# Softmax attention and a soft mixture of experts on one core: x turned in a slot's first half, denominators and product of x amid the second half's scores, maxima turned ahead of q and k

## The chip, the core and the metric

The kernel runs on one core of a Trainium2 chip. The time is the device time of one execution in microseconds (us). The core has five engines that run their own instructions in order and wait for each other by semaphores: PE (TensorE, matrix products into PSUM), ACT (ScalarE), DVE (VectorE), POOL (GpSimd, which here also issues most DMAs) and SP.

## The reference

```python
scores = scale * q @ k.T                     # 8 batches, 12 heads, 448 tokens, 64 wide
m = max(scores, -1)
e = exp(scores - m)
attn = e / (sum(e, -1) + exp(-m) + 1e-9)     # a softmax with one more term in the denominator
x = (attn @ v), heads side by side           # 3584 tokens x 768
logits = x @ phi                             # 32 slots
d = softmax(logits, 0); c = softmax(logits, 1)
out = c @ experts(d.T @ x)                   # 8 experts, relu(. @ w1[e]) @ w2[e]
```

## The kernel before

**Pairs and slots.** The 96 heads are worked on as 48 pairs; the two heads of a pair (hl = 0, 1) lie in partitions 0 to 63 and 64 to 127. After a ramp written out by hand, the loop at L751 has one slot for each pair s, with two halves (y = 0, 1). All order on the engines is the order of the program (a manual schedule); nothing is reordered.

**What is done to a pair n.** T(n) (L243, quads L270) turns q and k with 28 64x64 transposes on PE; ACT copies q out of PSUM, DVE copies k. A(n, i) makes the scores of 128 queries, and DVE takes the maximum over keys (L303, L313, L321) into wm. When the maxima of a group of three pairs are there, W2 turns them on PE (three products 128 wide and two into 64 partitions, L328 and L330), and W3 copies them (mT, L336) and makes exp(-m) in two instructions (ec, L340 and L343). Bk(n, i) makes the transposed scores of key block i, adds minus the maximum with a second product (sel times mT, L365, L394), and ACT takes exp (L367, L397). Inside Bk, in the steps form at L370, the products of A for a pair some slots ahead stand between those of Bk. AV (L431) multiplies with v, whose extra column of ones gives the sums: 64 queries of each head, the tail, go into separate halves of the partitions (shape 128x64), the rest in 128x128. N1 (L444) copies the result into ubuf on ACT. N2 adds exp(-m) to the sums on DVE (L459), takes the reciprocal (L460), and POOL multiplies (L464, L474, L475) into x. PX (L496) turns x on PE with four 128x128 products, and ACT copies it (L502).

**A slot before.** First half: Bk(s, 0), Bk(s, 1), AV of pair s-1 for key blocks 2 and 3, the work of the expert routing listed in post, the tail of AV(s-1), N1(s-1). Second half: Bk(s, 2), Bk(s, 3), T(s+6), in every third slot W2 and W3, AV(s) for key blocks 0 and 1, post, PX(s-2), and N2(s-1). So the product of a pair is started at the end of one slot, and x is turned at the end of the next.

**What else is in the queues.** POOL also does V (copies of v into its layout, L403 to L406), issues the loads of q, k, v and the weights (L176, L179, L183, L184, L113), and does parts of the routing (c_sub L572, d_sub L586, the scaling of acc L602). V and the loads of v come at the end of slots with s % 3 = 0, those of q and k with s % 3 = 2. The routing of a batch element repeats every six slots: l_mm (L530) in the first half of slots with s % 6 = 2, its maxima in slots 2 and 3, exps and corr in slot 4, s_mm (L618) in the second half of slots with s % 6 = 0. W2 falls in the second half of slots 2 and 5.

**Buffers.** PSUM has three banks for psA (scores for the maxima, turned k, routing), four for psB (scores, turned q, turned maxima, turned x), and one for psV (AV).

Of the kernel before, what the change touches and what calls it, by code (L numbers as in the profile page):

```python
# [31 lines left out]
def kernel(  # L32
# [123 lines left out]
    with ExitStack() as at:  # L156
# [86 lines left out]
        def T(n):  # L243
            g, pl = divmod(n, NP)
            if n >= NP * NP:
                quads(n, g, pl)
                return
            ps = psB.tile([128, 2, S], BF16, tag="b", name="ps_t")

            k0 = [psB.tile([128, 2, S], BF16, tag="b", name="ps_k") for _ in range(2)] if n == 0 else None  # L250
            for a in range(2):
                src = nat["qk"[a], g]
                order = [(tok, hl) for tok in range(7) for hl in range(2)]
                if a and n == 0:
                    order.sort(key=lambda z: kcol(z[1], z[0]))
                for tok, hl in order:
                    c = kcol(hl, tok) if a else (2 * tok if tok < 4 else 2 * tok - 7) * 64
                    r = slice(64 * hl, 64 * hl + 64)
                    o = k0[c // 256][r, 0, c:c + 64] if a and n == 0 else ps[r, a, c:c + 64]
                    nc.tensor.transpose(o, src[r, pl, tok * D:(tok + 1) * D], ident[r, r])  # L260
            t = qk_t[n % NQK]
            if n == 0:
                nc.scalar.copy(t[:, 0, :], ps[:, 0, :])
                nc.vector.tensor_copy(t[:, 1, 0:256], k0[0][:, 0, 0:256])
                nc.vector.tensor_copy(t[:, 1, 256:S], k0[1][:, 0, 256:S])
            else:
                nc.scalar.copy(t, ps)
            qkT[n] = t

        def quads(n, g, pl):  # L270

            pss = [p.tile([128, S], BF16, tag=tag, name="ps_t") for p, tag in ((psB, "b"), (psA, "a"))]
            for tok in range(7):
                for z in range(2):
                    for a in range(2):
                        hl = (z + a) % 2
                        r, o = slice(64 * z, 64 * z + 64), slice(64 * hl, 64 * hl + 64)
                        c = kcol(hl, tok) if a else (2 * tok if tok < 4 else 2 * tok - 7) * 64
# [3 lines left out]
            nc.vector.tensor_copy(t[:, 1, :], pss[1])  # L282
            qkT[n] = t
# [11 lines left out]
        def A(n, i, steps=False):  # L295
            t = qkT[n]
            if steps:

                def run(hl):
                    r = slice(64 * hl, 64 * hl + 64)  # L300
                    ps = psA.tile([128, 512], F32, tag="a", name="ps_a")
                    nc.tensor.matmul(ps[:, 0:S], t[r, 0, i * 128:(i + 1) * 128], t[r, 1, :], start=True, stop=True)  # L302
                    nc.vector.reduce_max(mcol(n, i, hl), ps[:, 0:S], axis=AX.X)  # L303

                return [lambda: run(0), lambda: run(1)]
            if i < 3:
                pss = [psA.tile([128, 512], F32, tag="a", name="ps_a") for _ in range(2)]
                for hl in range(2):
                    r = slice(64 * hl, 64 * hl + 64)
                    nc.tensor.matmul(pss[hl][:, 0:S], t[r, 0, i * 128:(i + 1) * 128], t[r, 1, :],  # L310
                                     start=True, stop=True)
                for hl in range(2):
                    nc.vector.reduce_max(mcol(n, i, hl), pss[hl][:, 0:S], axis=AX.X)  # L313
            else:
                ps = psA.tile([128, 512], F32, tag="a", name="ps_a")

                for hl in range(2):
                    r = slice(64 * hl, 64 * hl + 64)
                    nc.tensor.matmul(ps[64 - 64 * hl:128 - 64 * hl, 0:S], t[r, 0, 384:448], t[r, 1, :],  # L319
                                     start=True, stop=True)  # L320
                nc.vector.reduce_max(mcol(n, 3), ps[:, 0:S], axis=AX.X)  # L321

# [1 line left out]
        def W2(g):  # L324
            w = wm[g % 2]
            ps = pb_("ps_m")
            for i in range(3):
                nc.tensor.matmul(ps[:, i * 128:(i + 1) * 128], w[:, i, :], ident, start=True, stop=True)  # L328
            for z in range(2):
                nc.tensor.matmul(ps[64 * z:64 * z + 64, 384:448], w[:, 3, 0:64], ident[:, 64 - 64 * z:128 - 64 * z],  # L330
                                 start=True, stop=True)
            st["ps_m"] = ps

        def W3(g):
            t = psm.tile([128, S], BF16, tag="mT", name="mT")
            nc.scalar.copy(t, st["ps_m"][:, 0:S])  # L336
            mT[g] = t
            e = psm.tile([128, NP, 7], F32, tag="ec", name="ec", bufs=3)
            w = wm[g % 2]
            nc.scalar.activation(e[:, :, 0:6].rearrange("p l (i h) -> p l i h", i=3),  # L340
                                 w[:, 0:3, :].rearrange("p i (h c) -> p c i h", h=2)[:, 0:NP],
                                 AF.Exp, scale=-scale)
            nc.scalar.activation(e[:, :, 6], w[:, 3, 0:NP], AF.Exp, scale=-scale)  # L343
            ec[g] = e


        def Bk(n, i, c=0, mix=False):
# [4 lines left out]
            if i < 3 and mix and runs and runs[0][1] < 3:  # L352
# [10 lines left out]

                def bias(hl):
                    nc.tensor.matmul(pss[hl][:, 0:S], sel[rs[hl], pl:pl + 1].to_broadcast([64, 128]),  # L365
                                     mT[mg(n)][rs[hl], :], start=False, stop=True)
# [24 lines left out]
                nc.tensor.matmul(outs[hl], t[rs[hl], 1, cols], t[rs[hl], 0, :], start=True, stop=False)  # L391
            As(c)
            for hl in range(2):
                nc.tensor.matmul(outs[hl], sel[rs[hl], pl:pl + 1].to_broadcast([64, m]), mT[mg(n)][rs[hl], :],  # L394
                                 start=False, stop=True)
            for p, e in zip(pss, es):
                nc.scalar.activation(e, p[:, 0:S], AF.Exp, scale=scale)  # L397
# [18 lines left out]
        def AV(n, i, qs):  # L416
# [6 lines left out]
            for u in qs:  # L423
                for hl in range(2):
                    if u < 3:
                        c0 = (2 * u + hl) * W65
                        o, qc = a[:, c0:c0 + W65], slice(u * 128, (u + 1) * 128)
                    else:
                        t, z = (av_half["ps"], 0) if n == NPAIR - 1 else (a, 6 * W65)
                        o, qc = t[64 - 64 * hl:128 - 64 * hl, z:z + W65], slice(384, 448)  # L430
                    nc.tensor.matmul(o, eT[n, i, hl][:, qc], vp[g % 2][:, 2 * pl + hl, i, 0:W65],  # L431
                                     start=(i == 0 and u == 0 and hl == 0) or (u == 3 and i == 0 and n == NPAIR - 1),
                                     stop=(i == 3), skip_group_check=True)

# [3 lines left out]
        def N1(n):  # L438
# [5 lines left out]
            (nc.scalar.copy if on_pool(n) else nc.vector.tensor_copy)(u, src)  # L444
            us[n] = u

        def N2(n):
            g, pl = divmod(n, NP)
            b, pb = divmod(n, PB)
            u = us[n]  # L450
            eng = nc.gpsimd if on_pool(n) else nc.vector
            rec = psm.tile([128, 7], F32, tag="rec", name="rec", bufs=3)
            e = ec[mg(n)][:, group[n][1], :]
            if n == NPAIR - 1:
                nc.vector.scalar_tensor_tensor(rec[:, 6:7], av_half["ps"][:, D:W65], 1e-9, e[:, 6:7],
                                               op0=ALU.add, op1=ALU.add)
                nc.vector.scalar_tensor_tensor(rec[:, 0:6], u[:, 0:6, D], 1e-9, e[:, 0:6], op0=ALU.add, op1=ALU.add)
            else:
                nc.vector.scalar_tensor_tensor(rec, u[:, :, D], 1e-9, e, op0=ALU.add, op1=ALU.add)  # L459
            nc.vector.reciprocal(rec, rec)  # L460
            x = xb[b % 2]
            c = pb * 128
# [251 lines left out]
        for word in ramp.split():  # L714
# [7 lines left out]
            elif op == "X":  # L722
                W2(*arg)
                W3(*arg)
            elif op == "V":
                AV(*arg, range(3))
            elif op == "H":
# [23 lines left out]
        for s in range(3, NPAIR + 1):  # L751
            for y in range(2):
                hs = 2 * s + y
                mix = len(runs) > 1 and runs[0][1] == 1 - y
                if mix:
                    Bk(s, 2 * y, mix=True)
                    Bk(s, 2 * y + 1, y, mix=True)
                else:
                    As(1)
                if mix:  # L760
# [9 lines left out]
                    for i in (2, 3):  # L770
                        AV(s - 1, i, range(3))
                else:
                    if s < NPAIR - 6:
                        T(s + 6)
                    if s and s + 1 in firsts:
                        W2(mg(s + 1))
                        W3(mg(s + 1))
                    if s < NPAIR:
                        for i in (0, 1):
                            AV(s, i, range(3))  # L780
                for f in post.get(hs, ()):
                    f()
                if y and 0 <= s - 2 < NPAIR - 2:
                    PX(s - 2)
                if y == 0:
                    if 0 <= s - 1:
                        for i in range(4):
                            AV(s - 1, i, [3])
                        if s == NPAIR:
                            PX(s - 2)  # L790
                        N1(s - 1)
                        if not on_pool(s - 1):
                            N2(s - 1)
                else:
                    if 0 <= s - 1 and on_pool(s - 1):
# [227 lines left out]
```

## Time and profile before

| what | us |
|---|---|
| median of 3 runs (298.39 to 298.96) | 298.4 |
| the profiled execution | 297.51 |
| its span, first to last instruction | 295.7 |
| PE busy | 270.1 |
| ACT busy | 254.0 |
| DVE busy | 247.7 |
| POOL busy | 190.0 |

A busy time is the union of an engine's instructions, each with its latency: on ACT and DVE the next instruction starts before the one ahead has ended, and a product on PE shows about 0.16 us of pipeline behind the time in which it streams. In this document the distance between the starts of two neighbouring instructions is therefore used as the time that one of them costs. Six slots of the steady part, by their first product (us from the span's start):

| slot | begins | long | what is special |
|---|---|---|---|
| 29 | 157.05 | 4.98 | W2 and W3 |
| 30 | 162.03 | 5.32 | s_mm |
| 31 | 167.35 | 4.35 | |
| 32 | 171.70 | 5.39 | l_mm; W2 and W3 |
| 33 | 177.09 | 4.67 | routing maxima |
| 34 | 181.76 | 4.33 | exps of the routing |

### The profile page before, as it was taken

The page shows a single profiled execution, that of the slowest core. Times are in us where ns is not written, and L with a number is a line of the kernel's source. Part 1 is how long each engine was busy: PE and PEld are TensorE (multiplying, and loading weights), DVE is VectorE, ACT ScalarE, POOL GpSimd, SP SyncE. Part 2 cuts the span into 40 slices and gives each one's busy share as a digit, 9 for nine tenths or more (in the row PEclk, how much of TensorE's full clock was granted, in tenths as well). Part 3 has the DMA queues.
Part 4 walks back from the last instruction along what each step waited for, and adds up shares of the span by engine and source line. Part 5 has one row for each costly group of instructions (what it writes and reads, how often), then busy time and mean ns, then how long its engine had stood idle before and what let it go on. Part 6 is the DMA issues. An engine that isn't in the chain of part 4 may idle for free.

```text
span 295.7 us, 12404 instructions
## 1 busy us (share of the span) xinstructions
PE 270.1 (91%) x5191; PEld 155.6 (53%) x5191; DVE 247.7 (84%) x591; ACT 254.0 (86%) x585; POOL 190.0 (64%) x349
## 2 busy tenths in 40 slices
PE   5999999999999999999999999998999999996820
PEld 4445555555565566555655565556555556662100
DVE  5999899999899989999999999998999665537840
ACT  4569999999999999999999999998999988337730
POOL 8682887978786988887788779876786543000000
PEclk9999999999999999999999999999999999998555
DMA  7999999999999999999999999999699979908997
GB/s 134 147 152 207 150 134 166 198 163 198 176 197 156 191 181 205 168 193 177 200 185 188 186 179 182 186 191 197 105 147 201 219 158 262 352 19 304 410 450 326
DMA packets 47223, 58.67 MB, mean 198 GB/s; under 512 B 3008, under 2 KB 40128, under 8 KB 46912
## 3 DMA queue, kind: packets, MB, share of 16 engines
q0 software_dynamic: 40512, 42.29, 90.4%
q1 hardware_dynamic: 6656, 15.60, 13.6%
q8 instruction: 40, 0.66, 0.8%
q14 instruction: 15, 0.12, 0.1%
HBM read 89.16 MB, written 15.14 MB: 353 GB/s over the span
## 4 chain that ended last, share of the span: by engine, by line
PE 64%; ACT 22%; DVE 5%; issue 3%; DMA 1%; DVEq 0%; ACTq 0%
PE ps_av L431 14%; PE ps_a L302 8%; PE ps_b L362 8%; PE ps_b L365 7%; ACT W L397 6%; ACT W L367 6%; PE ps_b L391 5%; ACT W L502 3%; PE ps_b L394 3%; ACT W L281 3%; PE ps_t L279 3%; PE ps_o L916 2%; DVE W L313 2%; PE ps_x L496 2%; PE ps_s L618 2%
## 5 line engine op out<-in xcount | busy, mean ns | idle before, releaser
L303 DVE TENSOR_REDUCE W<-ps_a 128x1 bf16<-128x448 f32 x250 | 138.4, 614 | 5.0 <-PE ps_a L302 2.2
L367 ACT ACTIVATE W<-ps_b 128x448 bf16<-128x448 f32 x250 | 125.9, 643 | 1.2 <-PE ps_b L365 1.0
L302 PE MATMUL ps_a<-W 64*128 64x448 bf16 x250 | 79.4, 352 | 1.0 <-DVE cm L557 1.0
L362 PE MATMUL ps_b<-W 64*128 64x448 bf16 x250 | 72.3, 352 | 1.4
L431 PE MATMUL ps_av<-W 128*128 128x65 bf16 (+1 forms) x1536 | 65.1, 196 | 0.8 <-ACT ubuf L444 0.6
L365 PE MATMUL ps_b<-mT,sel 64*128 64x448 bf16 x250 | 65.0, 350 | 0.5
L431 PEld LDWEIGHTS <-W 128*128 128x128 bf16 (+1 forms) x1536 | 50.2, 100 | 27.8 <-issue 23.4
L464 POOL TENSOR_TENSOR W<-ubuf,rec 128x384 bf16<-128x384 f32 x44 | 36.3, 824 | 38.6 <-DVE rec L460 20.5
L397 ACT ACTIVATE W<-ps_b 128x448 bf16<-128x448 f32 x86 | 48.7, 607 | 2.5 <-PE ps_b L394 2.5
L502 ACT CAST W<-ps_x 128x512 bf16<-128x512 f32 x47 | 31.4, 667 | 2.3 <-PE ps_x L496 2.0
L365 PEld LDWEIGHTS <-sel 64*128 64x128 bf16 x250 | 19.2, 94 | 21.8 <-issue 14.4
L321 DVE TENSOR_REDUCE W<-ps_a 128x1 bf16<-128x448 f32 x48 | 29.6, 616 | 0.8 <-PE ps_a L319 0.8
L444 ACT COPY ubuf<-ps_av 128x455 f32<-128x455 f32 x44 | 27.7, 630 | 0.2
L113 POOL DMA_DIRECT2D W<-in_moe_w_dram x30 | 22.6, 756 | 8.0 <-PE ps_b L394 7.7
L302 PEld LDWEIGHTS <-W 64*128 64x128 bf16 x250 | 22.8, 94 | 8.8
L391 PE MATMUL ps_b<-W 64*64 64x448 bf16 (+1 forms) x134 | 26.4, 371 | 0.3 <-ACT W L502 0.2
L281 ACT COPY W<-ps_t 128x448 bf16<-128x448 bf16 x39 | 25.7, 658 | 0.0
L394 PE MATMUL ps_b<-mT,sel 64*64 64x448 bf16 (+1 forms) x134 | 24.7, 353 | 0.0
L279 PEld LDWEIGHTS <-W 64*64 64x64 bf16 x1092 | 20.1, 108 | 8.4 <-issue 2.0
L313 DVE TENSOR_REDUCE W<-ps_a 128x1 bf16<-128x448 f32 x38 | 21.1, 615 | 1.6 <-PE ps_a L310 1.4
L475 POOL TENSOR_TENSOR W<-ubuf,rec 128x128 bf16<-128x128 f32 x44 | 17.5, 398 | 3.7
L496 PE MATMUL ps_x<-ident,W 128*128 128x128 bf16 x192 | 18.7, 219 | 0.2 <-ACT W L472 0.2
(154 smaller groups left out, 460.6 us busy)
## 6 DMA issues: line engine op xcount, KB each, us to landing
W<-in_moe_w_dram POOLq DMA_DIRECT2D x24, 768.0 KB, 9.3
W<-in_v_dram POOLq DMA_DIRECT2D x32, 192.0 KB, 5.9
out_dram<-W SPq DMA_DIRECT2D x2, 2688.0 KB, 9.1
W<-in_q_dram POOLq DMA_DIRECT2D x15, 336.0 KB, 6.6
W<-in_k_dram POOLq DMA_DIRECT2D x26, 168.0 KB, 6.7
stage<-in_moe_w_dram POOLq DMA_DIRECT2D x4, 768.0 KB, 9.5
W<-stage SPq DMA_DIRECT2D x4, 576.0 KB, 6.7
out_dram<-W SPq DMA_DIRECT2D x6, 384.0 KB, 2.7
```

Source lines behind the costliest of these rows:

```text
L281: nc.scalar.copy(t[:, 0, :], pss[0])
L302: nc.tensor.matmul(ps[:, 0:S], t[r, 0, i * 128:(i + 1) * 128], t[r, 1, :], start=True, stop=True)
L303: nc.vector.reduce_max(mcol(n, i, hl), ps[:, 0:S], axis=AX.X)
L362: nc.tensor.matmul(pss[hl][:, 0:S], t[rs[hl], 1, cols], t[rs[hl], 0, :], start=True, stop=False)
L365: nc.tensor.matmul(pss[hl][:, 0:S], sel[rs[hl], pl:pl + 1].to_broadcast([64, 128]), mT[mg(n)][rs[hl], :], start=False, stop=True)
L367: nc.scalar.activation(e[:, hl, :], pss[hl][:, 0:S], AF.Exp, scale=scale)
L391: nc.tensor.matmul(outs[hl], t[rs[hl], 1, cols], t[rs[hl], 0, :], start=True, stop=False)
L394: nc.tensor.matmul(outs[hl], sel[rs[hl], pl:pl + 1].to_broadcast([64, m]), mT[mg(n)][rs[hl], :], start=False, stop=True)
L397: nc.scalar.activation(e, p[:, 0:S], AF.Exp, scale=scale)
L431: nc.tensor.matmul(o, eT[n, i, hl][:, qc], vp[g % 2][:, 2 * pl + hl, i, 0:W65], start=(i == 0 and u == 0 and hl == 0) or (u == 3 and i == ...
L464: eng.tensor_mul(x[:, 0:3, c:c + 128].rearrange("p i (h d) -> p i h d", h=2), u[:, 0:6, 0:D].rearrange("p (i h) d -> p i h d", h=2), rec[: ...
L502: nc.scalar.copy(xT(b, pb), pss[0])
```

## The change

1. In a slot's first half PX(s-2) now stands behind the tail of AV(s-1) and N1(s-1); before it was the last product of the second half.
2. N2 is split into den (L459) and mul (reciprocal and the POOL instructions). While there are maxima to be taken, den(s-1) stands between Bk(s, 2) and Bk(s, 3), and mul(s-1) right behind Bk(s, 3), ahead of T, post and PX.
3. W2 and W3 stand ahead of T instead of behind it. The two products of the tail maxima are 128x128 as the other three; for this the second head's q columns begin with the tail, so that the two heads read mT with an offset of 64, and mT is 512 wide instead of 448.
4. exp(-m) is one instruction (W4) instead of two. It is at the end of the next slot's first half, in the ramp and for the last group right behind W3 or T.

```diff
+        qcol = lambda hl, tok: (2 * tok if tok < 4 else 2 * tok - 7) * 64 if hl == 0 else (2 * tok + 1) * 64 if tok < 3 else (2 * tok - 6) * 64
+        def qcs(hl, i):
+            a = 128 * i + 64 * hl if i < 3 else 384 * (1 - hl)
+            return slice(a, a + (128 if i < 3 else 64))
...
         def W2(g):
             for i in range(3):
-                nc.tensor.matmul(ps[:, i * 128:(i + 1) * 128], w[:, i, :], ident, start=True, stop=True)
-            for z in range(2):
-                nc.tensor.matmul(ps[64 * z:64 * z + 64, 384:448], w[:, 3, 0:64], ident[:, 64 - 64 * z:128 - 64 * z],
-                                 start=True, stop=True)
+                nc.tensor.matmul(ps[:, 64 + i * 128:192 + i * 128], w[:, i, :], ident, start=True, stop=True)
+            for hl in range(2):
+                c, h = 448 * (1 - hl), 64 - 64 * hl
+                nc.tensor.matmul(ps[:, c:c + 64], w.rearrange("p i c -> p (i c)")[:, 384 - 64 * hl:512 - 64 * hl],
+                                 ident[:, h:h + 64], start=True, stop=True)
         def W3(g):
-            t = psm.tile([128, S], BF16, tag="mT", name="mT")
-            nc.scalar.copy(t, st["ps_m"][:, 0:S])
+            t = psm.tile([128, 512], BF16, tag="mT", name="mT")
+            nc.scalar.copy(t, st["ps_m"])
...
+        def W4(g):
+            e = psm.tile([128, NP, 8], F32, tag="ec", name="ec", bufs=3)
+            nc.scalar.activation(e.rearrange("p l (i h) -> p i h l", i=4),
+                                 wm[g % 2].rearrange("p i (h c) -> p i h c", h=2)[:, :, :, 0:NP], AF.Exp, scale=-scale)
...
+                early_den = y and on_pool(s - 1)
                 if mix:
                     Bk(s, 2 * y, mix=True)
+                    if early_den:
+                        den(s - 1)
                     Bk(s, 2 * y + 1, y, mix=True)
+                    if early_den:
+                        mul(s - 1)
+                        early_den = False
...
-                    if s < NPAIR - 6:
-                        T(s + 6)
                     if s and s + 1 in firsts:
                         W2(mg(s + 1))
                         W3(mg(s + 1))
+                    if s < NPAIR - 6:
+                        T(s + 6)
+                    if s + 1 == firsts[-1]:
+                        W4(mg(s + 1))
...
-                if y and 0 <= s - 2 < NPAIR - 2:
+                if y == 0:
+                    for i in range(4):
+                        AV(s - 1, i, [3])
+                    if s < NPAIR:
+                        N1(s - 1)
                     PX(s - 2)
...
                     if not on_pool(s - 1):
                         N2(s - 1)
+                    if 3 < s < firsts[-1] and s in firsts:
+                        W4(mg(s))
+                elif early_den:
+                    N2(s - 1)
```

More of the change, by code (lines that the diff above doesn't have):

```diff
@@ L256, in T @@
                 for tok, hl in order:
-                    c = kcol(hl, tok) if a else (2 * tok if tok < 4 else 2 * tok - 7) * 64
+                    c = (kcol if a else qcol)(hl, tok)
                     r = slice(64 * hl, 64 * hl + 64)
@@ L277, in quads @@
                         r, o = slice(64 * z, 64 * z + 64), slice(64 * hl, 64 * hl + 64)
-                        c = kcol(hl, tok) if a else (2 * tok if tok < 4 else 2 * tok - 7) * 64
+                        c = (kcol if a else qcol)(hl, tok)
                         nc.tensor.transpose(pss[a][o, c:c + 64], nat["qk"[a], g][r, pl, tok * D:(tok + 1) * D], ident[r, r])
@@ L301, in run @@
                     ps = psA.tile([128, 512], F32, tag="a", name="ps_a")
-                    nc.tensor.matmul(ps[:, 0:S], t[r, 0, i * 128:(i + 1) * 128], t[r, 1, :], start=True, stop=True)
+                    nc.tensor.matmul(ps[:, 0:S], t[r, 0, qcs(hl, i)], t[r, 1, :], start=True, stop=True)
                     nc.vector.reduce_max(mcol(n, i, hl), ps[:, 0:S], axis=AX.X)
@@ L309, in A @@
                     r = slice(64 * hl, 64 * hl + 64)
-                    nc.tensor.matmul(pss[hl][:, 0:S], t[r, 0, i * 128:(i + 1) * 128], t[r, 1, :],
+                    nc.tensor.matmul(pss[hl][:, 0:S], t[r, 0, qcs(hl, i)], t[r, 1, :],
                                      start=True, stop=True)
@@ L318, in A @@
                     r = slice(64 * hl, 64 * hl + 64)
-                    nc.tensor.matmul(ps[64 - 64 * hl:128 - 64 * hl, 0:S], t[r, 0, 384:448], t[r, 1, :],
+                    nc.tensor.matmul(ps[64 - 64 * hl:128 - 64 * hl, 0:S], t[r, 0, qcs(hl, 3)], t[r, 1, :],
                                      start=True, stop=True)
@@ L327, in W2 @@
             for i in range(3):
-                nc.tensor.matmul(ps[:, i * 128:(i + 1) * 128], w[:, i, :], ident, start=True, stop=True)
-            for z in range(2):
-                nc.tensor.matmul(ps[64 * z:64 * z + 64, 384:448], w[:, 3, 0:64], ident[:, 64 - 64 * z:128 - 64 * z],
-                                 start=True, stop=True)
+                nc.tensor.matmul(ps[:, 64 + i * 128:192 + i * 128], w[:, i, :], ident, start=True, stop=True)
[3 more added lines that the diff above has]
+                                 ident[:, h:h + 64], start=True, stop=True)
             st["ps_m"] = ps
         def W3(g):
-            t = psm.tile([128, S], BF16, tag="mT", name="mT")
-            nc.scalar.copy(t, st["ps_m"][:, 0:S])
+            t = psm.tile([128, 512], BF16, tag="mT", name="mT")
+            nc.scalar.copy(t, st["ps_m"])
             mT[g] = t
[L338 to L343, printed above, removed]
+        def W4(g):
+            e = psm.tile([128, NP, 8], F32, tag="ec", name="ec", bufs=3)
+            nc.scalar.activation(e.rearrange("p l (i h) -> p i h l", i=4),
+                                 wm[g % 2].rearrange("p i (h c) -> p i h c", h=2)[:, :, :, 0:NP], AF.Exp, scale=-scale)
             ec[g] = e
@@ L365, in bias @@
                     nc.tensor.matmul(pss[hl][:, 0:S], sel[rs[hl], pl:pl + 1].to_broadcast([64, 128]),
-                                     mT[mg(n)][rs[hl], :], start=False, stop=True)
+                                     mT[mg(n)][rs[hl], 64 - 64 * hl:64 - 64 * hl + S], start=False, stop=True)
                     nc.scalar.activation(e[:, hl, :], pss[hl][:, 0:S], AF.Exp, scale=scale)
@@ L393, in Bk @@
             for hl in range(2):
-                nc.tensor.matmul(outs[hl], sel[rs[hl], pl:pl + 1].to_broadcast([64, m]), mT[mg(n)][rs[hl], :],
+                nc.tensor.matmul(outs[hl], sel[rs[hl], pl:pl + 1].to_broadcast([64, m]), mT[mg(n)][rs[hl], 64 - 64 * hl:64 - 64 * hl + S],
                                  start=False, stop=True)
@@ L426, in AV @@
                         c0 = (2 * u + hl) * W65
-                        o, qc = a[:, c0:c0 + W65], slice(u * 128, (u + 1) * 128)
+                        o = a[:, c0:c0 + W65]
                     else:
                         t, z = (av_half["ps"], 0) if n == NPAIR - 1 else (a, 6 * W65)
-                        o, qc = t[64 - 64 * hl:128 - 64 * hl, z:z + W65], slice(384, 448)
-                    nc.tensor.matmul(o, eT[n, i, hl][:, qc], vp[g % 2][:, 2 * pl + hl, i, 0:W65],
+                        o = t[64 - 64 * hl:128 - 64 * hl, z:z + W65]
+                    nc.tensor.matmul(o, eT[n, i, hl][:, qcs(hl, u)], vp[g % 2][:, 2 * pl + hl, i, 0:W65],
                                      start=(i == 0 and u == 0 and hl == 0) or (u == 3 and i == 0 and n == NPAIR - 1),
@@ L445, in N1, with den @@
             us[n] = u
+        recs = {}
         def N2(n):
-            g, pl = divmod(n, NP)
-            b, pb = divmod(n, PB)
+            den(n)
+            mul(n)
+        def den(n):
             u = us[n]
-            eng = nc.gpsimd if on_pool(n) else nc.vector
-            rec = psm.tile([128, 7], F32, tag="rec", name="rec", bufs=3)
-            e = ec[mg(n)][:, group[n][1], :]
+            rec = recs[n] = psm.tile([128, 7], F32, tag="rec", name="rec", bufs=3)
+            e = ec[mg(n)][:, group[n][1], 0:7]
             if n == NPAIR - 1:
@@ L459, in N2, with mul @@
                 nc.vector.scalar_tensor_tensor(rec, u[:, :, D], 1e-9, e, op0=ALU.add, op1=ALU.add)
+        def mul(n):
+            b, pb = divmod(n, PB)
+            u, rec = us[n], recs.pop(n)
+            eng = nc.gpsimd if on_pool(n) else nc.vector
             nc.vector.reciprocal(rec, rec)
@@ L724 @@
                 W3(*arg)
+                W4(*arg)
             elif op == "V":
@@ L782 @@
                     f()
-                if y and 0 <= s - 2 < NPAIR - 2:
-                    PX(s - 2)
[L785 to L790, printed above, removed]
+                if y == 0:
[3 more added lines that the diff above has]
+                        N1(s - 1)
+                    PX(s - 2)
+                    if s == NPAIR:
                         N1(s - 1)
[L792 to L795, printed above, removed]
+                    if not on_pool(s - 1):
                         N2(s - 1)
+                    if 3 < s < firsts[-1] and s in firsts:
+                        W4(mg(s))
+                elif early_den:
+                    N2(s - 1)
                 if y == 0 and wait_loads:
```

## The prediction

> **What bounds the kernel now.** I read the page first. Its busy row shows four engines near full at once, so no single one's work gives the time:
>
> ```profile
> PE 270.1 (91%) x5191; PEld 155.6 (53%) x5191; DVE 247.7 (84%) x591; ACT 254.0 (86%) x585; POOL 190.0 (64%) x349
> ```
>
> Next the waits of each engine: PE's are short (1.4 us the longest in all), and POOL's are for `rec` (20.5 us), so POOL looks free. Then the timeline by engine in the steady part, slots 32 to 35. A slot's tail point, below, is where PE has ended the tail of AV and goes on: 174.41, 179.34, 183.88 and 188.53 us. PE in slots 34 and 35:
>
> ```profile
> 182.88 0.35 PE L302 MATMUL ps_a<-W 64*128 64x448 bf16 x1
> 183.16 0.79 PE L431 MATMUL ps_av<-W 128*128 128x65 bf16 x20
> 183.88 0.36 PE L302 MATMUL ps_a<-W 64*128 64x448 bf16 x1
> ...
> 185.34 0.54 PE L431 MATMUL ps_av<-W 128*128 128x65 bf16 x12
> 185.72 0.22 PE L622 MATMUL ps_ct<-ident,cd 128*128 128x128 bf16 x1
> 185.77 0.39 PE L496 MATMUL ps_x<-ident,W 128*128 128x128 bf16 x4
> 186.09 0.36 PE L302 MATMUL ps_a<-W 64*128 64x448 bf16 x1
> ```
>
> and DVE between slots 33 and 34:
>
> ```profile
> 181.11 0.61 DVE L321 TENSOR_REDUCE W<-ps_a 128x1 bf16<-128x448 f32 x1
> 181.64 0.38 DVE L282 COPY W<-ps_t 128x448 bf16<-128x448 bf16 x1
> 181.94 0.15 DVE L459 SCALAR_TENSOR_TENSOR rec<-ubuf,ec 128x7 f32<-128x7 f32 x1
> 182.13 0.20 DVE L460 RECIPROCAL rec<-rec 128x7 f32<-128x7 f32 x1
> 182.25 3.23 DVE L303 TENSOR_REDUCE W<-ps_a 128x1 bf16<-128x448 f32 x6
> ```
>
> The starts close a ring. The fourth scores of a first half (182.88) reuse the psA bank of the first, so they follow its reduce (182.25) by 0.63. From there PE takes 0.28 to AV and 0.72 to the tail point (183.88), where the first scores of the second half stand. Their reduce begins 0.45 later (the fifth of the six: 0.49 and three times 0.53 after 182.25). DVE then needs two reduces (1.06), the third (0.53), the copy of k (0.30), the denominator (0.19) and the reciprocal (0.12), 2.20 in all, until the first reduce of the next slot. 0.63 + 0.28 + 0.72 + 0.45 + 2.20 = 4.28, and slot 34 takes 4.33. ACT's jobs in such a slot, by distance of starts, are seven exps at 0.42, N1 0.42, q 0.41 and x 0.47: 4.26. So ring and ACT are level, and the dearer slots are longer by their own PE work or by what W3 adds to ACT.
>
> POOL is another matter. This is its timeline over slots 32 to 35:
>
> ```profile
> 176.61 0.41 POOL L572 TENSOR_TENSOR z<-lb,cm 128x128 f32<-128x128 f32 x1
> 177.72 0.82 POOL L464 TENSOR_TENSOR W<-ubuf,rec 128x384 bf16<-128x384 f32 x1 [0.70 <-DVE rec L460]
> ...
> 179.37 0.82 POOL L176 DMA_DIRECT2D W<-in_q_dram  x1
> ...
> 181.94 0.79 POOL L113 DMA_DIRECT2D W<-in_moe_w_dram  x1
> ...
> 184.28 0.66 POOL L403 COPY W<-W 128x576 bf16<-128x576 bf16 x1
> ...
> 187.75 0.66 POOL L602 TENSOR_TENSOR acc<-acc,corr 128x224 f32<-128x224 f32 x1
> 188.37 0.82 POOL L464 TENSOR_TENSOR W<-ubuf,rec 128x384 bf16<-128x384 f32 x1
> 189.54 0.40 POOL L475 TENSOR_TENSOR W<-ubuf,rec 128x128 bf16<-128x128 f32 x1
> ```
>
> From the product of pair 31 (177.72) to the end of that of pair 33 (189.94) it has no idle time. PX(33) begins at 190.75, 0.81 later: all the slack there is.
>
> **The change, part by part.**
>
> PX in the first half. Four turns last 0.32 (185.77 to 186.09) and now stand in the ring, behind the tail point: 0.63 + 0.28 + 0.72 + 0.32 + 0.42 + DVE. On DVE the denominator no longer stands just ahead of the reciprocal that waits for it (0.12 for 0.19; the trace has no denominator followed by a reduce, so 0 to 0.19): 2.13. The ring becomes 4.50, 0.22 more than now, in every slot that it bounds. In the second half AV(s) now meets the scores itself. Where AV is followed by another shape its 12 products take 0.466, where by PX 0.375: PE has one more switch of shape in a slot, 0.09 us.
>
> The Trainium skill's page TensorEngine Tiling (Array Packing), section Tiling Modes, says "Changing tiling mode (not just tile) drains the TensorE", which speaks against this part. The trace agrees (0.466 against 0.375); with PE alone setting the end it would be the first rival below.
>
> Maxima ahead of q and k. B3 to W2, W2 to T and T to AV are three switches; T to W2, to its 128x64 products, to AV were three too: nothing on PE. On ACT, W3 goes from 0.42 to that of a copy 512 wide, 0.47, and two exps (0.13 + 0.09) become one, between 0.13 and 0.23, taken as 0.14, in the next first half: less by 0.03, 17 times, 0.5 us at most. What helps is the order: today x's copy waits behind W3 and both exps, and the next first half's scores take 1.73 to 1.80 instead of 1.40 because the fourth psB bank is x's.
>
> Now the six intervals between tail points from slot 29 on, today and then:
> - 29 to 30 (W2): 5.06; then ACT bounds with N1, x, seven exps, W3, q = 4.72, taken as 4.70.
> - 30 to 31 (s_mm): 4.98; PE's 0.32 + 0.65 + 0.40 + 0.35 + 0.38 + 0.70 + 0.09 = 2.89, then 0.42 + 0.63 + 0.28 + 0.72 = 4.94.
> - 31 to 32 (l_mm, 0.59 in the ring): 4.88; 4.50 + 0.59 = 5.08.
> - 32 to 33 (W2): 4.93; PE's 0.32 + 0.65 + 0.50 + 0.31 + 0.35 + 0.38 + 0.23 = 2.74, then 0.42 + 0.63 + 0.28 + 0.78 = 4.85.
> - 33 to 34: 4.54; ring with 0.12 of s_max in DVE's way, 4.62.
> - 34 to 35: 4.65; ring with the copy of L623, 4.63.
>
> 29.04 becomes 28.82: 0.2 less in six slots, if x's products are in time.
>
> The products on POOL. Today mul starts when the reciprocal is out, 3.16 behind slot 32's tail point. Then: PX 0.32, first reduce 0.42, two reduces 1.06, denominator 0.12, third reduce 0.53, reciprocal 0.20 = 2.65, so 0.51 earlier. But c_sub (176.61), which POOL does today while it waits, then stands behind the product: +0.43. Everything from the q load on is unchanged and without a gap, so pair 33's product ends at 189.94 - 0.51 + 0.43 = 189.86. PX(33) moves from 190.75 to slot 35's tail point, 174.41 + 4.85 + 4.62 + 4.63 = 188.51. **PE waits 1.4 us** with the semaphore. Behind PX stand N1's copy of x on ACT, all second-half scores, their reduces and exps: nothing covers it, and the next slots, near their bounds, can't give it back. The same sum for pairs 21 and 27 gives 1.4 each, with their gapless queues. Pair 39 (no loads of q): 0.9. Pair 9 (no L602): 0.7. Pair 3: 0.4. Pair 15, where the q load waits 1.11 for something else: 1.4 to 2.4, taken as 1.9. Pair 43 in the tail: 0.5. Products that aren't behind V's and q's queue: pair 31's has 0.45 to spare and pair 30's 0.5. Sum: 0.4 + 0.7 + 1.9 + 4.2 + 0.9 + 0.5 = 8.6. Against it 0.2 in some six periods: -1.2.
>
> Net +7.4. The profiled execution took 297.5 (1.8 around its span of 295.7), so 304.9; the median of the runs is 0.9 above it: **305.8 us**.
>
> **The rivals.**
> - PE alone (0.10): the ring is loose, because DVE's order changes and reduces catch up, and products come in time as the slots stretch. Then 0.09 of shape switch in some 42 slots is 3.8: 302.2. For it: PE busy 28.73 of 29.04 us in slots 29 to 34. Against it: its waits are hidden as long first stages of scores.
> - ACT's relief wins (0.10): the one way to a faster kernel. x's copy leaves the second half, and the first stages of 1.73 to 1.80 fall to 1.40 twice in six slots: 0.37 x 13 = 4.8, 293.6. It decides only where POOL ends the third pair's product before the tail point; its gapless 10.6 us from 179.37 speak against it.
> - The change doesn't do what it says (0.06): the reciprocal comes no earlier, held by ec or by scores behind PX; then the stall has 0.51 more in six places: 308.8.
> - Gains and stalls cancel (0.04): 298.4.
> - The forecast has 0.70.
>
> **How the numbers follow.** Lower end of the forecast's own bounds: the stalls stay, but the three intervals without them fall to ACT's 4.26 to 4.7, some 14.0 instead of 14.7: 4 us less over the periods, 301.5. Upper end: every stall full and 0.2 of ring in the intervals that I hold at ACT's bound, 311. The range reaches down to the case of no change: 298.2 to 311.0, and leaves out the faster rival and the forecast's ends. Some 0.6 us (0.2%) is what a measurement can tell from no change. Faster 0.10, same 0.04, slower 0.86.
>
> **What would show it.** In the profile after: PE waiting at L496 for POOL's x, about 1.4 us in slots 11, 17, 23, 29, 35 (a wait that today doesn't exist); first-half scores after a W2 slot at about 1.4 instead of 1.8; plain slots near 4.5; AV of the second half at 0.47. If PE has no such wait, the forecast is wrong, most likely because POOL's work between two products is placed otherwise than I read it. If the waits are there and the total is under 301, it is the rows of the ring that are wrong.

## The result, and the profile after

The changed kernel takes 303.6 us (median of 4 runs, 303.19 to 304.43) where the kernel before took 298.7 beside it (median of 4, 298.39 to 300.55): a ratio of 1.0142, 95% interval 1.0099 to 1.0185. Ratios, here and below, are worked out from the fast executions alone, as some others of the same kernels ran in a slower state. The ratio differs from the quotient of the two medians, 1.0165, which lies inside the interval. The kernel is slower, as forecast, and inside the range; the forecast of 305.8 was 2.2 us too high. The profiled execution took 304.4, the longest of the four.

The busy row of the page, and the chain of work that ended last, followed back from the last instruction:

```profile
PE 273.2 (90%) x5191; PEld 160.8 (53%) x5191; DVE 246.8 (82%) x591; ACT 255.6 (84%) x568; POOL 189.6 (63%) x349
...
PE 64%; POOL 14%; ACT 5%; DVE 5%; issue 4%; DMA 3%; DVEq 0%; POOLq 0%; ACTq 0%
```

The chain of the kernel before was:

```profile
PE 64%; ACT 22%; DVE 5%; issue 3%; DMA 1%; DVEq 0%; ACTq 0%
```

POOL does the same work as before, and is now in 14% of the chain where it had no share. In the view of the line that turns x (L510 in the new numbering), products and weight loads together, idle time in us and how often:

```profile
  POOL W L489: 6.9, 15
  POOL W L478: 2.0, 7
```

PE and its weight load show the same wait twice here, so these are not to be added. The starts of the phases on PE give what it costs: PX takes 0.33 where it doesn't wait, and the tail 0.25. Above that are 0.43 for pair 9, 0.77 for pair 14, 1.05 for 15, 0.79 each for 21, 27 and 33, 0.71 for 39, and 0.27 for two others together: 5.6 us. Slot 35 on PE:

```profile
192.73 0.79 PE L437 MATMUL ps_av<-W 128*128 128x65 bf16 x20
193.65 0.34 PE L510 MATMUL ps_x<-ident,W 128*128 128x128 bf16 x3
194.41 0.23 PE L510 MATMUL ps_x<-ident,W 128*128 128x128 bf16 x1 [0.41 <-POOL W L489]
194.57 0.36 PE L308 MATMUL ps_a<-W 64*128 64x448 bf16 x1
```

AV and its tail would end at 193.44. The first three turns wait for the large product of x (L478, out at 193.59), the fourth for the small one (L489, out at 194.35), and only then come the second half's scores. POOL in the same time, from the product of pair 31 to that of pair 33:

```profile
181.81 0.82 POOL L478 TENSOR_TENSOR W<-ubuf,rec 128x384 bf16<-128x384 f32 x1 [1.72 <-DVE rec L474]
...
183.35 0.40 POOL L586 TENSOR_TENSOR z<-lb,cm 128x128 f32<-128x128 f32 x1
183.69 0.82 POOL L176 DMA_DIRECT2D W<-in_q_dram  x1
...
192.77 0.82 POOL L478 TENSOR_TENSOR W<-ubuf,rec 128x384 bf16<-128x384 f32 x1
...
193.96 0.40 POOL L489 TENSOR_TENSOR W<-ubuf,rec 128x128 bf16<-128x128 f32 x1
```

It is the queue of before, with c_sub now behind the product, and pair 33's product ends 0.9 us behind the place in which PE wants it.

### The profile page after: what moved, and what is told of

Same layout as the page of the kernel before. It is cut to its first block, busy times and chain, and to the rows that moved or that the text cites. A ratio compares the mean times of both kernels' runs of the same rounds, so it can differ in the third digit from the quotient of the medians.

```text
span 302.6 us, 12387 instructions
## 1 busy us (share of the span) xinstructions
PE 273.2 (90%) x5191; PEld 160.8 (53%) x5191; DVE 246.8 (82%) x591; ACT 255.6 (84%) x568; POOL 189.6 (63%) x349
## 4 chain that ended last, share of the span: by engine, by line
PE 64%; POOL 14%; ACT 5%; DVE 5%; issue 4%; DMA 3%; DVEq 0%; POOLq 0%; ACTq 0%
PE ps_av L437 13%; PE ps_a L308 9%; PE ps_b L368 6%; PE ps_b L371 6%; PE ps_b L397 4%; PE ps_x L510 4%; DMA W<-in_k_dram 3%; POOL W L478 3%; PE ps_t L285 3%; PE ps_b L400 3%; PE ps_o L939 3%; DVE W L319 2%; PE ps_s L632 2%; PE ps_h L876 2%; PE ps_l L544 2%
## 5 line engine op out<-in xcount | busy, mean ns | idle before, releaser
L309 DVE TENSOR_REDUCE W<-ps_a 128x1 bf16<-128x448 f32 x250 | 140.6, 619 | 14.7 <-PE ps_a L308 13.3
L373 ACT ACTIVATE W<-ps_b 128x448 bf16<-128x448 f32 x250 | 121.6, 587 | 3.4 <-PE ps_b L371 3.3
L308 PE MATMUL ps_a<-W 64*128 64x448 bf16 x250 | 81.6, 351 | 0.8 <-DVE W L327 0.7
L368 PE MATMUL ps_b<-W 64*128 64x448 bf16 x250 | 67.3, 353 | 0.0
L478 POOL TENSOR_TENSOR W<-ubuf,rec 128x384 bf16<-128x384 f32 x44 | 36.1, 821 | 44.0 <-DVE rec L474 32.9
L403 ACT ACTIVATE W<-ps_b 128x448 bf16<-128x448 f32 x86 | 46.9, 586 | 2.0 <-PE ps_b L400 2.0
L516 ACT CAST W<-ps_x 128x512 bf16<-128x512 f32 x47 | 29.5, 628 | 5.1 <-PE ps_x L510 5.0
L327 DVE TENSOR_REDUCE W<-ps_a 128x1 bf16<-128x448 f32 x48 | 29.7, 619 | 0.7 <-PE ps_a L325 0.7
L371 PEld LDWEIGHTS <-sel 64*128 64x128 bf16 x250 | 22.2, 94 | 12.0 <-issue 3.4
L450 ACT COPY ubuf<-ps_av 128x455 f32<-128x455 f32 x44 | 25.6, 582 | 0.2
L510 PE MATMUL ps_x<-ident,W 128*128 128x128 bf16 x192 | 21.0, 226 | 3.7 <-POOL W L489 2.7
L287 ACT COPY W<-ps_t 128x448 bf16<-128x448 bf16 x39 | 23.9, 612 | 0.0
L319 DVE TENSOR_REDUCE W<-ps_a 128x1 bf16<-128x448 f32 x38 | 21.1, 618 | 1.6 <-PE ps_a L316 1.4
L489 POOL TENSOR_TENSOR W<-ubuf,rec 128x128 bf16<-128x128 f32 x44 | 17.5, 398 | 3.7
L285 PEld LDWEIGHTS <-W 64*64 64x64 bf16 x1092 | 15.5, 108 | 6.1 <-DMA W<-in_k_dram 0.9
```

The costliest lines, as they stand in the source:

```text
L308: nc.tensor.matmul(ps[:, 0:S], t[r, 0, qcs(hl, i)], t[r, 1, :], start=True, stop=True)
L368: nc.tensor.matmul(pss[hl][:, 0:S], t[rs[hl], 1, cols], t[rs[hl], 0, :], start=True, stop=False)
L478: eng.tensor_mul(x[:, 0:3, c:c + 128].rearrange("p i (h d) -> p i h d", h=2), u[:, 0:6, 0:D].rearrange("p (i h) d -> p i h d", h=2), rec[: ...
L510: nc.tensor.matmul(pss[i // 2 if two else 0][:, o:o + 128], x[:, i, c], ident if i < 3 else ident2, start=True, stop=True)
```

## The experiments

There are four theories of the loss: POOL (PE waits for x's product, which POOL's queue makes late), SHAPE (PE changes the shape of its products once more in each slot), RING (PX makes the loop of PE and DVE longer) and PARTS (the other two parts of the change cost the time). What each expects stands with each run. All ratios are to the kernel before, run on the same chip, with 95% intervals. "Six slots" is taken from the profiled execution: the intervals between the starts of the second half's first scores in neighbouring slots, the median of slots 10 to 40 for each slot number modulo 6, and the sum of these six. It is 29.05 us before and 29.99 after the change. It comes from one execution of each kernel, so it is a help beside the ratio and has no interval.

| kernel | ratio | interval | six slots |
|---|---|---|---|
| change | 1.0142 | 1.0099 to 1.0185 | 29.99 |
| maxima alone | 0.9961 | 0.9928 to 0.9995 | 28.90 |
| denominators alone | 1.0012 | 0.9977 to 1.0048 | 28.95 |
| both, PX where it was | 0.9935 | 0.9893 to 0.9977 | 28.80 |
| PX alone | 1.0454 | 1.0381 to 1.0528 | 31.40 |
| change, PX one pair earlier | 1.0027 | 0.9982 to 1.0073 | 29.16 |
| change, loads of v later | 1.0059 | 1.0019 to 1.0099 | 29.73 |
| change, PX between blocks 2 and 3 | 1.0039 | 1.0003 to 1.0074 | 29.36 |
| the same, loads of v later | 1.0001 | 0.9965 to 1.0036 | 29.31 |
| PX one pair earlier, ahead of the tail | 0.9995 | 0.9962 to 1.0029 | 29.31 |
| both, PX between block 3 and T | 0.9963 | 0.9933 to 0.9992 | 29.10 |
| PX one pair earlier, one denominator later | 1.0023 | 0.9982 to 1.0065 | 29.26 |

### PX back in its place

```diff
+                if y and 0 <= s - 2 < NPAIR - 2:
+                    PX(s - 2)
...
-                    if s < NPAIR:
-                        N1(s - 1)
-                    PX(s - 2)
...
```

> The changed kernel with PX back where it was, last in the second half; early denominators and products and the turned maxima stay. Theory POOL (PE waits for x's product because PX stands 2 us earlier in the program while POOL's queue is as long as before): no wait at PX, and the extra shape switch and the longer ring go too, so 298.0 us or less, 296 to 298.5. Rival SHAPE (the loss is the shape switch of 0.09 us in each slot, some 3.8 us): also gone here, 299 to 300, since the rest of the loss is then the other two parts'. Rival PARTS (early denominators or the maxima cost the time): stays over 301.

297.1 us, 0.9935. No wait of PX for POOL is left, and the kernel is faster than before. With the other parts in, the loss comes from PX's place; PARTS falls.

### PX for one pair earlier

```diff
+        def turned(s):
+            if s == 3 or s >= NPAIR - 4:
+                return [] if s == 3 else [s - 2]
+            return [s - 3, s - 2] if s % PB == 1 else [] if s % PB == 2 else [s - 3]
...
-                    PX(s - 2)
+                    for z in turned(s):
+                        PX(z)
```

> The changed kernel with PX at its new place, but for the pair before: x of pair s-3 is turned in slot s (in slots with s % 6 = 1 also pair s-2, in slots with s % 6 = 2 none, so that the routing finds its x; from slot 44 on as in the change). Same number of products, same shape switches, same place on PE; only the wait for POOL goes. POOL: the waits at PX seen in the changed kernel's trace sum to 5.6 us, so 298.0 (297 to 299.5). SHAPE: nothing changes, 303 to 304. Rival RING (PX between the tail of AV and the next scores makes the loop of PE and DVE longer): 303.

300.2 us, 1.0027, where the kernel before took 299.4 beside it; POOL's 297 to 299.5 is missed. Place and shapes are the change's, only the product is an old one (in one slot of six two pairs are turned, in another none), and of 1.42% there remain 0.27%: by the ratios the wait for POOL is 3.4 us of the loss, less than the 5.6 that the waits sum to. In six slots 0.83 us go, where one stall took 0.79. PE in the slot that waited before:

```profile
191.24 0.79 PE L437 MATMUL ps_av<-W 128*128 128x65 bf16 x20
191.96 0.40 PE L510 MATMUL ps_x<-ident,W 128*128 128x128 bf16 x4
192.29 0.36 PE L308 MATMUL ps_a<-W 64*128 64x448 bf16 x1
```

0.33 from PX to the next scores, for 0.92 in the change. SHAPE and RING as the main cause fall. But 1.0027 against 0.9935 stays: another 2.7 us, without any late product. In six slots it is 0.36 (29.16 for 28.80). Not all of it need be PX's place: of the 4.3 us between the spans of the two profiled executions 0.9 lie ahead of slot 4, where this kernel waits twice for loads of k, 0.63 us each, and the one with PX in its old place once, 0.52. Whether the other executions have such waits isn't shown.

### PX alone

```diff
-                if y and 0 <= s - 2 < NPAIR - 2:
-                    PX(s - 2)
...
                         N1(s - 1)
+                        if s < NPAIR:
+                            PX(s - 2)
```

> The kernel before with PX alone moved to the first half, behind N1; denominators and product at the end of the second half as before, maxima behind q and k. POOL: products start some 0.4 us later than in the changed kernel, so the waits are longer by that in six or seven places and x's product is late in more slots: 306 to 309, with PE waiting 1.2 us or more at PX in slots 11, 17, 23, 29, 35. SHAPE: as the changed kernel or less, 302.4. ACT relief without stalls: under 298.

313.1 us, 1.0454: more than expected. The place is as expected (PE in slot 29):

```profile
167.85 0.79 PE L431 MATMUL ps_av<-W 128*128 128x65 bf16 x20
168.90 0.34 PE L496 MATMUL ps_x<-ident,W 128*128 128x128 bf16 x3 [0.26 <-POOL W L464]
169.65 0.23 PE L496 MATMUL ps_x<-ident,W 128*128 128x128 bf16 x1 [0.41 <-POOL W L475]
169.81 0.36 PE L302 MATMUL ps_a<-W 64*128 64x448 bf16 x1
```

The tail could end at 168.57 (AV and tail 0.72), so PE loses 0.9 here, not 1.2. But there are more such slots. What the line that turns x waits for in this kernel (us, times; products and weight loads together):

```profile
  POOL W L475: 10.1, 24
  POOL W L464: 4.7, 12
```

By the starts on PE, as above, the waits at PX sum to 9.8 of the 13.7 us lost: 0.9 each for pairs 15, 21, 27, 33 and 39, 1.34 for pair 14, 0.80 for pair 30, 0.3 to 0.5 for pairs 3, 8, 9, 20, 26, 32 and 43, and less for some others. So x's product is late in more slots, as POOL expected. Where the other 3.9 us go isn't worked out. Moving only the consumer costs three times what moving it with its producer does.

### The turned maxima alone

```diff
-                    if s < NPAIR - 6:
-                        T(s + 6)
                     if s and s + 1 in firsts:
                         W2(mg(s + 1))
                         W3(mg(s + 1))
+                    if s < NPAIR - 6:
+                        T(s + 6)
```

(with the new W2, W3, W4 and q's columns of the change)

> The kernel before with the turned maxima alone: W2 and W3 ahead of T, one shape, one exp in the next first half; PX, denominator and product where they were. Forecast by the trace: first scores after a slot with W2 fall from 1.8 us towards 1.4, some 0.2 to 0.3 us in each of 13 such slots, so 295 to 297.5. If the maxima ahead of T make DVE's or ACT's part late instead: 299 to 301. POOL says nothing of it.

298.0 us, 0.9961: a gain, but 0.15 us in six slots, where 0.2 to 0.3 in each of two intervals had been expected. The two intervals that hold W2 (slots with s % 6 = 2 and 5, by the medians) fall from 4.93 to 4.82 and from 5.06 to 4.92, and that of slots with s % 6 = 3 rises from 4.53 to 4.64.

### The loads of v a slot later

```diff
-                    load(g - 1, "v")
+                    v_later.append(g - 1)
...
+            if s > 3 and s % 3 == 1 and v_later:
+                load(v_later.pop(), "v")
```

> The changed kernel with POOL's queue shortened instead of PX moved: the two loads of v (0.73 + 0.72 us of POOL) are issued a slot later, behind the product that they delayed; PX, denominators, product and maxima as in the change. POOL: the products of pairs 9, 15, 21, 27, 33 and 39 end 1.45 us sooner, more than the 0.8 that PE waits for each, so the waits go and the time falls to that of the kernel with PX for one pair earlier, a ratio of 1.000 to 1.006 (299 to 301 where the kernel before takes 299.4). SHAPE and RING: nothing of theirs changes, 1.012 or more.

300.9 us, 1.0059. PX isn't moved; POOL's queue ahead of the product is 1.4 us shorter, and most of the wait goes:

```profile
189.66 0.35 POOL L412 COPY W<-W 64x192 bf16<-64x192 bf16 x1
190.09 0.66 POOL L616 TENSOR_TENSOR acc<-acc,corr 128x224 f32<-128x224 f32 x1
190.81 0.83 POOL L478 TENSOR_TENSOR W<-ubuf,rec 128x384 bf16<-128x384 f32 x1
...
191.99 0.40 POOL L489 TENSOR_TENSOR W<-ubuf,rec 128x128 bf16<-128x128 f32 x1
```

The product is out at 192.39 and PX begins at 192.67. Pair 14 still waits, 0.81 by the starts; pairs 15, 21, 27, 33 and 39 no longer do. Shown from the producer's side: it is POOL's queue.

### PX between the scores of blocks 2 and 3

```diff
                     Bk(s, 2 * y, mix=True)
+                    if y:
+                        PX(s - 2)
                     if early_den:
                         den(s - 1)
```

> The changed kernel with PX between the scores of key blocks 2 and 3 instead of ahead of block 2. PX has as many shape switches around it as in the change (one more a slot than before), but the first scores of the second half are issued ahead of it, so it no longer stands in the loop of PE and DVE; and it comes 0.67 us later, so of the 0.8 us that PE waits some 0.1 stays. RING: 0.992 to 0.998. SHAPE: the switches stay, 1.001 to 1.004.

299.7 us, 1.0039: where SHAPE put it (1.001 to 1.004), and clear of RING's 0.992 to 0.998. But here some products may still be late, so the next kernel takes the loads of v away too.

> The same with the loads of v a slot later too, so that no product is late and only the place of PX tells. RING: 0.990 to 0.996, as the kernel with PX in its old place (0.9935). SHAPE: 1.001 or more, as the kernel with PX for one pair earlier (1.0027).

299.3 us, 1.0001: between the two theories. The loop itself shows in DVE's wait for scores (us, times, longest), first of the change, then with PX for one pair earlier, then of this kernel:

```profile
DVE W L309 <- PE ps_a L308: 13.3, 37, 1.2
```

```profile
DVE W L309 <- PE ps_a L308: 7.6, 30, 0.5
```

```profile
DVE W L309 <- PE ps_a L308: 2.2, 5, 0.9
```

The 13.3 holds the late products too; without them it is 7.6, and from slot 10 to 40 nearly all of that is 0.18 to 0.41 right behind PX in four slots of six. (With PX in its old place the sum is 7.6 as well, but mostly at other places in the slot.) So RING is right that PX stood in the loop. With the loop free, the time isn't told apart from that of PX one pair earlier (1.0027), and it is still 0.66% over that with PX at the end.

### PX ahead of the tail of AV

```diff
+                    for z in turned(s) if s < NPAIR - 4 else []:
+                        PX(z)
                     for i in range(4):
                         AV(s - 1, i, [3])
```

> The kernel with PX for one pair earlier, and PX ahead of the tail of AV instead of behind it: next to products of its own shape, so the additional shape switch is gone, 0.09 us a slot on PE and in the loop of PE and DVE; PX's other 0.23 us stay in the loop, and N1 comes later by them. SHAPE: 3.8 us less, 0.990. RING: of the 0.22 us by which the loop is longer 0.09 goes where it bounds, some 1.5 to 2.5 us, 0.994 to 0.999.

298.6 us, 0.9995: 0.32% less than behind the tail, within both intervals; just above RING's 0.994 to 0.999, whose upper end its interval holds, and clear of SHAPE's 0.990.

### PX between block 3 and T

```diff
                     if s and s + 1 in firsts:
                         W2(mg(s + 1))
                         W3(mg(s + 1))
+                    if s < NPAIR:
+                        PX(s - 2)
                     if s < NPAIR - 6:
                         T(s + 6)
```

> The kernel with early denominators and turned maxima and PX in the second half (0.9935), with PX between the scores of block 3 and T instead of last: two more shape switches a slot (64x64 to 128x128 to 64x64), 0.19 us of PE, no late product, and the copy of k, whose cover on DVE is 0.2 to 0.3 us, hardly later. SHAPE (a switch that PE must do anyway is paid in full): 0.19 x 40 = 7.6 us, 1.019. If a switch costs half, as the kernel with PX between blocks 2 and 3 had it (1.0001): 1.005 to 1.008. If switches are free and place is all: 0.993.

297.7 us, 0.9963, 0.28% or 0.8 us more than with PX last, within both intervals. The 7.6 us expected for SHAPE counted too much: in every third slot W2's 128x128 products stand between block 3 and T anyway, and PX adds no switch there. In the other slots both switches are there: the scores of block 3 take 0.498 where 0.403, and AV ahead of the next scores 0.47 where 0.38. That is 0.19 in some 26 slots, 4.9 us, and 0.76 in six slots, of which the six slots of the table show 0.30 (29.10 for 28.80). So SHAPE falls as a price that is paid in full; how much of it is hidden, the ratios can't tell.

Another difference between the places is what ACT has to do while PE makes the first scores of the next slot. ACT about the end of a second half, in the change and then with PX last:

```profile
191.37 0.58 ACT L287 COPY W<-ps_t 128x448 bf16<-128x448 bf16 x1
191.98 1.85 ACT L373 ACTIVATE W<-ps_b 128x448 bf16<-128x448 f32 x4
```

```profile
186.27 0.60 ACT L287 COPY W<-ps_t 128x448 bf16<-128x448 bf16 x1
186.68 0.68 ACT L516 CAST W<-ps_x 128x512 bf16<-128x512 f32 x1
187.16 1.96 ACT L373 ACTIVATE W<-ps_b 128x448 bf16<-128x448 f32 x4
```

Behind q's copy, which costs 0.41 between starts, the change waits 0.20 for the exps' scores; with PX last, x's copy fills the time. This wait stands in four intervals of six of the change (0.17 to 0.52). Behind q's copy ACT waits 0.67 us in slots 29 to 34 with PX last, 0.97 with PX between block 3 and T, 1.01 between blocks 2 and 3 and 1.37 one pair earlier behind the tail. That is the order of the times (0.9935, 0.9963, 1.0001, 1.0027), but no run changed this wait alone, so as a cause it isn't shown.

### The denominators alone, and one of them later

```diff
+                    if early_den:
+                        den(s - 1)
                     Bk(s, 2 * y + 1, y, mix=True)
+                    if early_den:
+                        mul(s - 1)
```

> The kernel before with early denominators and products alone; PX and the maxima as before. DVE loses 0.07 us a slot (the reciprocal no longer waits for the denominator), products are sooner than PX needs them: 0.994 to 1.000. POOL: PX is not earlier, so no wait, no loss. If the parts were not independent and this part were the costly one: over 1.003.

298.8 us, 1.0012: no difference that this can tell, and just above the 0.994 to 1.000 that was expected.

In the change the denominators of slots 21, 27 and 33 take 0.48 to 0.49 us, for 0.16 elsewhere. In slot 33:

```profile
185.87 0.49 DVE L468 SCALAR_TENSOR_TENSOR rec<-ubuf,ec 128x7 f32<-128x7 f32 x1
186.28 0.61 DVE L327 TENSOR_REDUCE W<-ps_a 128x1 bf16<-128x448 f32 x1
```

while POOL does d_sub:

```profile
185.79 0.54 POOL L600 TENSOR_TENSOR z<-lb,lb 128x160 f32<-128x160 f32 x1
```

```diff
-                    if early_den:
+                    if early_den and s % PB != 3:
                         den(s - 1)
```

> The kernel with PX for one pair earlier (1.0027), with the denominator behind block 3's maximum, next to its reciprocal, in slots with s % 6 = 3 alone. There it took 0.48 us instead of 0.15 in the traces, beside POOL's d_sub. If DVE waits for POOL's operation: the interval after those slots' tail point falls from 4.86 by 0.2 to 0.3, in seven places, 1.5 to 2 us, 0.996 to 0.999. If the long denominator was hidden or is only how the trace shows it: 1.001 to 1.004.

299.1 us, 1.0023: not told apart from 1.0027. The kernel that this is compared with, PX one pair earlier, has the long denominator in two slots alone, 21 and 33, not in seven. There the denominator takes 0.15 again and the interval falls from 4.85 to 4.65, while the next rises by 0.10. In slots 15, 27 and 39, where the denominator took 0.15 to 0.22 before this edit, the interval rises from 4.59, 4.52 and 4.52 to 4.65. So the long denominator costs time where it stands, and this edit takes some in the slots that didn't have it.

### Both parts without the move, with more rounds

> The kernel with early denominators, products and turned maxima and PX in its old place, once more with more rounds, to tell whether it beats the kernel before. POOL and the forecast of the six intervals without stalls (28.82 for 29.04 in six slots, some 1.3 us in all) give 0.995 to 0.996; its first measurement was 0.9935. If that was the chip's scatter: 0.998 to 1.002.

The edit is that of PX back in its place. 298.3 us beside 299.2, 0.9947 (0.9911 to 0.9983): the gain is there again, about half a per cent. Early denominators, products and turned maxima with PX left in its place beat both kernels.

## Why the prediction was right, point by point

- **The main step, PE waits for x's product, was right in its place and its cause.** Waits stand in slots 11, 17, 23, 29, 35 and 41, and in 16 (pair 14, which I had passed over); the wait forecast for pair 3 didn't come. Taking the wait away from the consumer's side leaves 0.27% of the 1.42%, and from the producer's side 0.59%.
- **The term that was mis-sized is the stall: 1.4 forecast, 0.79 measured** in three of the slots, 5.6 against 8.6 in all. Of the 0.6, 0.30 is that the three intervals ahead of it take 14.40, not 14.10; 0.14 that pair 33's product ends 15.31 behind slot 32's tail point, not 15.45; 0.17 that only the last of the four turns waits for the product's end, so that 0.16 of PX stands behind it and not 0.33.
- **The intervals without the stall were too short by 0.5 in six slots** (29.29 from slot 29's tail point to slot 35's in the change, less its stall of 0.79, for 28.82). W2's 4.70 came out at 4.72, and s_mm's 4.94 at 5.08. Slot 33's 4.62 was 4.86: there the long denominator stood in the loop, a cost of nothing in my sum (in slot 39, where it takes 0.16, the interval is 4.53).
- **That the sum was near is in part luck.** The gain of 1.2 wasn't there: outside the stalls the profiled execution is 1.3 us longer than that of before. In the forecast the stalls were 3.0 us too long and the rest 2.5 too short, which leaves 0.5: the profiled execution was to take 304.9 and took 304.4. The other 1.7 of the 2.2 us come from the last step, which put the median 0.9 above the profiled execution, as before; this time it lies 0.8 below it.
- **The sign in the first-half scores was half misread.** Before, only one of the two slots behind W2 has scores of 1.80 (slot 30; slot 33 has 1.47), and the 1.73 stands in slots 29 and 35. In the change slots 30 and 33 have 1.36, and 29 and 35 have 1.34; but slot 34's rose from 1.40 to 1.83, behind the long denominator, and slot 32's from 1.40 to 1.57.
- **The reciprocal earlier by 0.51, c_sub behind the product by 0.43**: 2.61 behind the tail point for 2.65, and c_sub stands at 183.35 as said.
- **The ring** was right as a mechanism (without late products DVE waits 7.6 us for scores with PX in the loop, 2.2 with PX behind them). The price of 0.22 in every slot that it bounds wasn't reached: the run with the loop freed differs from the one with the loop by 0.26%, 0.8 us, which the intervals don't tell from nothing.
- **The switch of shape**: 0.466 for 0.375 is there in the second half, as read. As a rival it fell: with every switch in place and no late product, 0.27% of the 1.42% is left. What part of the 2.7 us below is the switch stays open.
- **Open**: how the 2.7 us between PX one pair earlier and PX last divide into loop, switch and ACT's wait. Single steps are 0.3 to 0.4%, no wider than the intervals, and part of it may lie ahead of slot 4.

## What to carry to other kernels

Before a consumer is moved up in an in-order program, take from the trace the time between its producer's end and its start for every instance, not the mean: POOL was 64% busy, yet one instance in six had 0.8 us to spare and was moved up by 2.2. Follow the producer's queue back to its last idle time; what counts is that length, and what the move puts into it. Moving the consumer and the other parts are separate edits; here the early denominators and the turned maxima together were worth keeping without the move (0.9935 and 0.9947). Of the two the maxima alone gained (0.9961), and the denominators alone showed no gain (1.0012).

## What the runs showed of the hardware

A denominator on DVE, which reads two SBUF operands (ubuf and ec), took 0.48 to 0.49 us instead of 0.16 in three slots of the change. Each time it began some 0.09 us behind a POOL operation on SBUF (d_sub) and ended 0.04 us behind it. In slot 9 the two began in the same 0.01 us, and it took 0.16. Beside POOL's DMA issues alone it took 0.16 to 0.17, but for one of 0.23. Moved off d_sub in slot 33 it took 0.15. That POOL's operation holds it up agrees with the Trainium skill's page SBUF — State Buffer, section SBUF: two separate sides, by which DVE and GpSimd share a pair of ports as an exclusive lock that also binds a DVE operation with two SBUF inputs against a GpSimd operation that reads SBUF: the trace agrees, with 0.33 us of waiting for an operation of 0.54.
